# Retention attention into a top-2 expert layer on one core: gathers paced by matmuls, tail casts behind the next pair's first k cast

## The chip, the core and the metric

The kernel is one program on one core of a Trainium2 chip. The metric is the time of one execution on the device in microseconds (us), given as the median of several runs. The engines that matter are TensorE (PE, matmuls and transposes), VectorE (DVE), ScalarE (ACT), GpSimd (POOL, which also issues all indirect DMAs) and SyncE (SP, which only issues DMAs). Each engine works through its own queue in order, and engines wait for each other by semaphores.

## The reference, cut

All inputs and the output are float32. q, k and v are [8 batches, 8 heads, 576 positions, 64]. Attention has a decay in place of a softmax; its output is the input x of a noisy top-2 router and an expert layer.

```python
scores = (1 / 8) * q @ k.T                      # per batch and head
gamma = 1.0 - 2.0 ** (-5.0 - arange(8))         # per head
ret = scores * where(rel >= 0, gamma ** rel, 0) # rel = query position - key position
x = (ret @ v).transpose(0, 2, 1, 3).reshape(4608, 512)

noisy = x @ w_gate + log1p(exp(x @ w_noise)) * noise     # 8 experts
top2, weights = the two largest of noisy, softmax over these two
for e in range(8):
    h = relu(x[rows of e] @ w1[e])              # 512 -> 1024
    out[rows of e] += weight * (h @ w2[e])      # 1024 -> 512
```

## The kernel before, in words

**A planner sets the order.** The whole program is first recorded as a list of operations (`op`), each with an engine or a choice of two, a cost in microseconds, a priority and its buffers. `Plan.run` is a list scheduler: it goes through planned time, takes operations that are ready by priority, gives them buffers (`slot`) and emits each engine's instructions in that planned order. On the chip each engine then follows its queue in this order; semaphores are set from the data dependencies. The planned costs decide the order and nothing else. Buffers come in classes: `xg` (24 buffers for gathered rows, of which the expert stream may use 14 while the routing stream still needs some), `half`, `big`, PSUM banks. When the other streams of a class are done, `slot` opens the class to the one that is left: for `xg` not all at once, but 5 buffers and then one more for every two allocations (`mark`); for the other classes at once.

**Attention** runs over 16 units (a pair of batches has four: two halves of the heads by two batches), each over 512 positions. `load` (L406) fetches k, q, v through SP; `cast` (L435) scales k to bf16 on ACT (L449) or DVE (L451), and q (L457) and v (L464) with the decay, mostly on POOL; `tr` (L469) transposes on PE (L482) and copies back (`copy`: L269 on ACT, L271 on DVE); `scores` (L488, matmuls L507, mask L515); `states` (L522, matmuls L542 and L544, copies to `tb` L554 on ACT); `out_` (L561, L581 and L591). The last 64 positions of all heads of a pair of batches are its **tail** (`tail`, L604): loads by `load_tail` (L424), a k cast (L614, ACT or DVE), q and v casts (L618, DVE or POOL), transposes, scores and output of its own. There are four tails.

**Routing** (`route`, L672) follows each pair of batches, so there are four. Each writes its rows of x to a DRAM buffer `xd` (L843) and makes the list of row numbers `xi` (L823) that the gathers go by.

**Expert tiles** (`tiles`, L923). Nine early tiles of at most two row blocks of 128 use what the first three routings have found; the rest, tiles of up to four blocks ("wide"), need the last routing. `fetch` (L954) makes the gathers on POOL (L964, one indirect DMA for each block of 128 rows), then transposes on PE (L982), or for experts 6 and 7 DMA transposes (L972). `up` (L1021, matmuls L1036) and `wide` (L1049, matmuls L1062) make the first layer, with the relu L1045 on ACT or L1047 on DVE; `second` (L1113) is the second layer's matmul. `wide` interleaves the first layer of a tile with the second layer of the tile before it.

**Results.** A row gets two experts. The first one's result goes to a DRAM buffer `yd` (L1147 scales it on ACT, L1153 writes it); at the second one's turn `prev` (L1116) gathers it back on POOL (L1128), DVE adds it (L1157), and POOL scatters the sum to the output (L1161). So POOL's queue holds gathers, result gathers, scatters and the weight loads that cast on the way (L900, L904, experts 0 to 2); experts 3 to 7 load through SP (L914, L917) and are cast on ACT or DVE.

**Priorities.** Attention has its unit's number, a tail u - 0.5, a routing u - 0.4, early tile i has 100 + 4i, and the wide tiles' fetches 100 + 4i - 2, two tiles ahead.

Of the kernel before, what the change touches and what calls it, by code (L numbers as in the profile page):

```python
# [17 lines left out]
P = 128  # L18
# [4 lines left out]
DM = 512  # L23
# [6 lines left out]
YOFF = [sum(min(-(-x // P) * P, CAP) for x in FIRST[:e]) for e in range(E + 1)]  # L30
WAIT = (11, 14, 15)
CROSS = 6
CLOSE = ((256, 0, 0, 0, 0, 0, 0, 0), (512, 384, 384, 0, 0, 0, 0, 0), (768, 640, 512, 0, 0, 0, 0, 0))
PLW = 8
XW = DM // 2 + PLW
# [13 lines left out]


class Op:
    __slots__ = ("i", "eng", "fn", "prio", "dma", "port", "preds", "succ", "need", "allocs", "bufs", "fin", "on")


class Plan:
# [5 lines left out]
    BIAS = dict(DVE=1.5, ACT=0.5)  # L61

    def __init__(self):
        self.ops, self.slots, self.fifo, self.quota, self.zone, self.mark = [], {}, {}, {}, {}, {}

    def cls(self, name, tiles, **quota):
        self.slots[name] = [[0.0, None, t, p] for t, p in tiles]
# [6 lines left out]
    def fix(t=None):  # L74
        return Buf(None, None, t)

    def op(self, eng, cost, fn, r=(), w=(), prio=0.0, dma=0, after=(), port=False):
        o = Op()
        o.i, o.fn, o.prio, o.dma, o.port = len(self.ops), fn, prio, dma, port
        o.eng = eng if isinstance(eng, dict) else {eng: cost}  # L80
        o.succ, o.allocs, o.bufs = [], [], []
        preds = set(after)
        for items, wr in ((r, False), (w, True)):
            for it in items:
                b, sub = it if isinstance(it, tuple) else (it, None)
                for s2, o2, w2 in b.acc:
                    if (wr or w2) and (sub is None or s2 is None or s2 == sub):
                        preds.add(o2)
                if b not in o.bufs:
                    o.bufs.append(b)  # L90
        for items, wr in ((r, False), (w, True)):
            for it in items:
                b, sub = it if isinstance(it, tuple) else (it, None)
                if wr:
                    b.acc = [a for a in b.acc if a[1] is o or not (sub is None or a[0] == sub)]
                b.acc.append((sub, o, wr))
        preds.discard(o)
        for b in o.bufs:
            if b.cls is not None:
                if not b.ops:  # L100
                    o.allocs.append(b)
                    self.fifo.setdefault((b.cls, b.stream), []).append(b)
                b.ops.append(o)
                b.left += 1
        o.preds, o.need = preds, len(preds)
        for p in preds:
            p.succ.append(o)
        self.ops.append(o)
        return o

    def run(self):
        free, dma_free, port = {}, {}, [0.0]
        head = {k: 0 for k in self.fifo}
        used = {}
        lanes = {"SP": [], "POOL": []}
# [4 lines left out]
        def slot(b, taken):  # L120
            s = self.slots[b.cls]
            lim = self.quota[b.cls].get(b.stream, len(s))
            lo, hi = self.zone.get((b.cls, b.stream), (0, len(s)))
            if lim < len(s) and all(head[k] >= len(v) for k, v in self.fifo.items()
                                    if k[0] == b.cls and k[1] != b.stream):
                lo, hi = 0, len(s)
                n = head[b.cls, b.stream]
                lim = min(hi, 5 + (n - self.mark.setdefault((b.cls, b.stream), n)) // 2) if b.cls == "xg" else hi
            if used.get((b.cls, b.stream), 0) + sum(t[1].n for t in taken if t[1].cls == b.cls) + b.n > lim:
                return None  # L130
            ok = lambda x: x[1] is None and all(x is not y for t in taken for y in t[0])
            best = None
            for i, x in enumerate(s[:hi]):
                if i < lo:
                    continue
                if b.n == 2:
                    if i % 2 or not (ok(x) and ok(s[i + 1])):
                        continue
                    c, k = [x, s[i + 1]], (max(x[0], s[i + 1][0]), 0)
                elif not ok(x):  # L140
                    continue
                else:
                    c, k = [x], (x[0] + (0.3 if len(s) == 8 and ok(s[i ^ 1]) else 0.0), 1)
                if best is None or k < best[0]:
                    best = k, c
            return best and best[1]

        while ready:
            pick = None
            for o in ready:  # L150
# [16 lines left out]
                if not ok:  # L167
                    continue
                t0 = max([y[0] for x, b in taken for y in x], default=0.0)
                best = None  # L170
                for e, c in o.eng.items():
                    t = max(t0, free.get(e, 0.0))
# [16 lines left out]
            ready.remove(o)  # L189
            o.on = e  # L190
            free[e] = t + c
            if o.port and e in ("DVE", "POOL"):
                port[0] = t + c
            o.fin = t + c
# [39 lines left out]
class Kernel:  # L234
# [200 lines left out]
    def cast(self, u):  # L435
# [9 lines left out]
        def k(e):  # L445
# [3 lines left out]
                nc.scalar.activation(o, i, Act.Copy, scale=0.125)  # L449
            elif e == "DVE":  # L450
                nc.vector.tensor_scalar_mul(o, i, 0.125)  # L451
        pl.op({"ACT": 1.06, "DVE": 0.7}, 0, k, r=[rk], w=[kn], prio=u, port=True)

        def q(e):
            i = rq.t.rearrange("p (h r d) -> p h r d", h=4, r=4)
# [148 lines left out]
    def tail(self, bp, prio):  # L604
# [2 lines left out]
        tab, maskt, ident = (self.fixed[x] for x in ("tab", "maskt", "ident"))  # L607
        raw = {n: d["raw" + n] for n in "qkv"}
        qk, vt = pl.buf("half", "tl"), pl.buf("half", "tl")
        h8 = lambda a: a.rearrange("p (h d) -> p h d", h=E)  # L610
        qv = lambda j: qk.t.bitcast(BF16)[:, j * DM:(j + 1) * DM]
        vv = lambda: vt.t.bitcast(BF16)[:, :DM]
        pl.op({"ACT": 0.63, "DVE": 0.6}, 0,
              lambda e: nc.scalar.activation(qv(1), raw["k"].t, Act.Copy, scale=0.125) if e == "ACT"  # L614
              else nc.vector.tensor_scalar_mul(qv(1), raw["k"].t, 0.125), r=[raw["k"]], w=[(qk, 1)], prio=prio, port=True)
        for j, n, o, b in ((8, "q", lambda: qv(0), (qk, 0)), (9, "v", vv, vt)):
            pl.op({"DVE": 0.69, "POOL": 1.06}, 0,
                  lambda e, j=j, n=n, o=o: self.eng(e).tensor_tensor(  # L618
                      h8(o()), h8(raw[n].t), tab.t[:, :, j:j + 1].to_broadcast([P, E, HD]), Alu.mult),
                  r=[raw[n], tab], w=[b], prio=prio, port=True)  # L620
        pt, TT = self.psum("tl"), pl.buf("half", "tl")

        def tr(e):
# [330 lines left out]
    def fetch(self, i, t, prio):  # L954
# [6 lines left out]
        rows = 1 + 1152 * (early + 1)  # L961
        for x, j in zip(xg, js):
            h, n = HPE * e + j, self.size(j)
            pl.op("POOL", 1.3, lambda _, x=x, h=h, n=n: nc.gpsimd.indirect_dma_start(  # L964
                out=x.t[:n, :], out_offset=None, in_=self.xd[:rows, :], in_offset=IOff(ap=xi.t[:n, h:h + 1], axis=0),
                bounds_check=rows - 1, oob_is_err=False), r=[xi] + self.xd_done[early], w=[x], prio=prio, dma=0.4)
        xT = pl.buf("half" if early < 3 else "big", "xt")
        w, m, off = sum(self.size(j) for j in js), len(js) * P, self.off(js)
        xv = lambda m=m: xT.t.bitcast(BF16)[:, :KD * m].rearrange("p (k s) -> p k s", k=KD)
# [79 lines left out]
    def wide(self, i, t, prio, g2=None):  # L1049

        pl, nc = self.pl, self.nc
        w, d = self.W[t[0]], self.t[i]
        n, xT, xv = d["w"], d["xT"], d["xv"]
        hT = d["hT"] = [pl.buf("half", "exp") for _ in range(4)]
        for f in range(KF):
            p = self.psum("exp")

            def pe(_, f=f, p=p):
                it = g2(f) if g2 else iter(())
                for di in range(KD):  # L1060
                    o = di * F + f * P
                    nc.tensor.matmul(p.t[:, :n], lhsT=w.t[:, o:o + P], rhs=xv()[:, di, :n],  # L1062
                                     start=(di == 0), stop=(di == KD - 1))
                    next(it, None)
                for _ in it:
                    pass
            r, ww, c = [xT] + [(w, k) for k in range(KD)], [p], 0.435 * n / 256
            if g2:
                r2, w2, c2 = g2.deps(f)
                r, ww, c = r + r2, ww + w2, c + c2  # L1070
            pl.op("PE", c, pe, r=r, w=ww, prio=prio)
            hv = lambda f=f: hT[f // 2].t.bitcast(BF16).rearrange("p (f s) -> p f s", f=2)[:, f % 2, :n]
            op = pl.op({"ACT": 0.17 + 0.00084 * n, "DVE": 0.1 + 0.00115 * n}, 0, lambda g, p=p, hv=hv: self.relu(
                g, hv(), p.t[:, :n]), r=[p], w=[(hT[f // 2], f)], prio=prio)
            if g2:
                for s in g2.ends(f):
                    self.finish(i - 1, g2.t, s, prio)
        return op
# [28 lines left out]
    def second(self, e, po, hT, c, f):  # L1107
# [2 lines left out]
        k = KF // len(hT)  # L1110
        hv = hT[f // k].t.bitcast(BF16).rearrange("p (f s) -> p f s", f=k)[:, f % k]
        o = KD * F + f * DM
        self.nc.tensor.matmul(po.t, lhsT=hv[:, c:c + P], rhs=self.W[e].t[:, o:o + DM],  # L1113
                              start=(f == 0), stop=(f == KF - 1))

    def prev(self, i, t, prio):  # L1116
        pl, nc = self.pl, self.nc
# [52 lines left out]

    def record(self):
        pl = self.pl
        self.u, self.tails, self.T, self.xT, self.W, self.t, self.keep, self.scats, self.wdma, self.inps = {}, {}, {}, {}, {}, {}, {}, {}, [], []
        self.setup()
        for u in range(3):
            self.load(u)
# [27 lines left out]
        for i, t in enumerate(ts):  # L1204
            starts.setdefault(t[0], i)
        last = {t[0]: i for i, t in enumerate(ts)}
        ne = len([t for t in ts if t[2] < 3])
        landed = lambda u: [o for o in pl.ops if o.dma and o.prio == u]
        for e, u in enumerate(WAIT):
            self.weights(e, 40 + e, True, landed(u))  # L1210
# [200 lines left out]
```

## Time and profile before

| | |
|---|---|
| median of 3 runs | 490.4 us (485.36, 490.4, 490.55) |
| the profiled execution's own time | 485.52 us |
| its span in the profile | 484.0 us |
| mean TensorE clock granted | 0.926 |
| busy: PE, DVE, ACT, POOL | 398.0 us (82%), 187.5 (39%), 246.4 (51%), 292.9 (61%) |
| gathers L964 on POOL | 80, of 1045 ns each |
| scatters L1161 and result gathers L1128 | 39 of 1003 ns, 39 of 1022 ns |
| matmuls L1062 and L1113 | 640 each, 190.5 us and 214.9 us busy |
| first matmul of a wide tile (L1062) | starts at 227.70 us |
| last matmul | ends at about 474 us |

A line of the profile names the kernel's line (L964), the engine, the instruction, and output and input by the program's names. "<-" in brackets or behind a bar names what ended the engine's idle time ahead of an instruction: an engine and its instruction, a DMA, "issue" (nothing that the profile shows), or "remote" (a semaphore update for which the profile finds no instruction). The clock is a share of TensorE's full speed.

### The profile page before, as it was taken

The numbers are of one execution on the slowest core, as the hardware profiler recorded it, in microseconds if no ns is written. First come the engines' busy times: TensorE is split into PE (matmuls) and PEld (weight loads), VectorE is DVE, ScalarE is ACT, GpSimd is POOL, SyncE is SP. The second block draws the span as 40 slices with busy tenths as digits, with TensorE's granted clock in tenths as the row PEclk, the third lists the DMA queues.
The fourth block names the chain that finished last, engine by engine and source line by source line (L and its number), as shares of the span: only waits on it lengthen the run. The fifth ranks groups of instructions, "written<-read, shape, count | busy, mean of one in ns | idle before, by whom it ended". The sixth has DMA issues, their size and how long they took to land. (4 is left out here: it accounts for less than half of the span.)

```text
span 484.0 us, 10610 instructions
## 1 busy us (share of the span) xinstructions
PE 398.0 (82%) x4032; PEld 245.5 (51%) x4032; DVE 187.5 (39%) x499; ACT 246.4 (51%) x431; POOL 292.9 (61%) x361
## 2 busy tenths in 40 slices
PE   1698768729988898149999888999799979999991
PEld 1576657528766665026565434455354434454450
DVE  2755776855892782001133313215025021031231
ACT  3699758657874743026575354745345233244320
POOL 8985779874497365733007747544656746656524
PEclk9889769878999999569999989999999979999997
DMA  7999999999599595423189977695599996645414
GB/s 192 298 261 286 272 238 303 257 245 328 128 319 269 136 256 166 96 75 118 37 291 349 343 248 220 188 369 166 167 310 298 236 217 182 181 150 161 150 55 144
DMA packets 102488, 105.32 MB, mean 218 GB/s; under 512 B 31870, under 2 KB 80511, under 8 KB 102434
## 3 DMA queue, kind: packets, MB, share of 16 engines
q1 hardware_dynamic: 80082, 58.92, 41.8%
q0 software_dynamic: 15264, 36.89, 30.2%
q10 hardware_dynamic: 7088, 8.80, 5.2%
q8 instruction: 32, 0.52, 0.5%
q14 instruction: 22, 0.18, 0.1%
HBM read 83.20 MB, written 26.63 MB: 227 GB/s over the span
## 5 line engine op out<-in xcount | busy, mean ns | idle before, releaser
L1113 PE MATMUL ps<-W,half 128*128 128x512 bf16 x640 | 214.9, 388 | 24.6 <-ACT half L1045 18.1
L1062 PE MATMUL ps<-big,W 128*128 128x512 bf16 (+4 forms) x640 | 190.5, 331 | 5.8 <-issue 5.2
L1045 ACT ACTIVATE half<-ps 128x512 bf16<-128x512 f32 (+5 forms) x180 | 87.1, 505 | 158.2 <-PE ps L1062 70.2
L964 POOL DMA_INDIRECT xg<-xd,xi x80 | 83.6, 1045 | 57.0 <-issue 20.4
L1113 PEld LDWEIGHTS <-half 128*128 128x128 bf16 x640 | 62.2, 99 | 99.4 <-ACT half L1045 18.9
L1062 PEld LDWEIGHTS <-W 128*128 128x128 bf16 x640 | 63.1, 99 | 55.5 <-issue 9.1
L1157 DVE SCALAR_TENSOR_TENSOR half<-ps,xg,half 128x512 f32<-128x512 f32 (+1 forms) x39 | 29.0, 747 | 73.5 <-PE ps L1113 42.1
L1161 POOL DMA_INDIRECT out_dram<-half,xg x39 | 39.1, 1003 | 29.6 <-issue 16.6
L1128 POOL DMA_INDIRECT half<-yd,xg x39 | 39.8, 1022 | 11.9 <-issue 11.9
L515 DVE TENSOR_TENSOR half<-ps,mask 128x512 bf16<-128x512 f32 x64 | 40.1, 682 | 16.4 <-PE ps L507 14.4
L269 ACT ACTIVATE half<-ps 128x1024 bf16<-128x1024 bf16 (+1 forms) x36 | 35.1, 990 | 15.5 <-PE ps L482 9.3
L457 POOL TENSOR_TENSOR half<-big,tab 128x1024 bf16<-128x1024 f32 x16 | 31.0, 1935 | 14.6 <-PE ps L482 6.2
L464 POOL TENSOR_TENSOR half<-big,tab 128x512 bf16<-128x512 f32 x32 | 33.6, 1066 | 1.5 <-issue 1.5
L542 PE MATMUL ps<-half,half 128*128 128x128 bf16 (+1 forms) x128 | 30.2, 322 | 2.4 <-POOL half L464 2.2
L1157 DVE SCALAR_TENSOR_TENSOR half<-ps,gm,half 128x512 f32<-128x512 f32 x6 | 4.5, 751 | 70.9 <-ACT half L1147 64.4
L1036 PE MATMUL ps<-half,W 128*128 128x256 bf16 (+1 forms) x288 | 29.1, 255 | 2.9 <-ACT half L269 2.5
L482 PE MATMUL ps<-ident__69,half 128*128 128x128 bf16 x256 | 22.3, 247 | 11.0 <-ACT half L449 5.9
L544 PE MATMUL ps<-vz,half 128*128 128x128 bf16 x128 | 25.4, 251 | 6.3 <-ACT vz L269 4.6
L1147 ACT ACTIVATE half<-ps,xg 128x512 f32<-128x512 f32 (+1 forms) x29 | 19.9, 685 | 16.4 <-PE ps L1113 11.0
L1036 PEld LDWEIGHTS <-W 128*128 128x128 bf16 x288 | 24.0, 98 | 7.0 <-issue 3.4
L554 ACT ACTIVATE tb<-ps 64x256 bf16<-64x256 f32 x56 | 21.1, 376 | 11.0 <-PE ps L544 9.8
L482 PEld LDWEIGHTS <-half 128*128 128x128 bf16 x256 | 18.9, 113 | 12.0 <-ACT half L449 5.9
(177 smaller groups left out, 462.8 us busy)
## 6 DMA issues: line engine op xcount, KB each, us to landing
big<-in_moe_w_dram SPq DMA_DIRECT2D x40, 512.0 KB
big<-in_k_dram SPq DMA_DIRECT2D x32, 256.0 KB
big<-in_q_dram SPq DMA_DIRECT2D x16, 512.0 KB
big<-in_v_dram SPq DMA_DIRECT2D x32, 256.0 KB
yd<-half SPq DMA_DIRECT2D x26, 256.0 KB
W<-in_moe_w_dram POOLq DMA_DIRECT2D x12, 512.0 KB
xd<-xg ACTq DMA_DIRECT2D x16, 264.0 KB
yd<-half ACTq DMA_DIRECT2D x15, 256.0 KB
```

The lines of the kernel that those rows point to most:

```text
L269: self.nc.scalar.activation(out, in_, Act.Copy)
L464: self.eng(e).tensor_tensor(o, i, t, Alu.mult)
L482: nc.tensor.transpose(v[:, hp, x, :], i[:, y, hp * P:(hp + 1) * P], ident.t)
L515: nc.vector.tensor_tensor(S.t.bitcast(BF16).rearrange("p (h c x) -> p h c x", h=2, c=2)[:, h], p[h].t.rearrange("p (c x) -> p c x", c=2), ...
L964: pl.op("POOL", 1.3, lambda _, x=x, h=h, n=n: nc.gpsimd.indirect_dma_start(out=x.t[:n, :], out_offset=None, in_=self.xd[:rows, :], in_offs ...
L1036: nc.tensor.matmul(pv()[:, f2, :], lhsT=w.t[:, o:o + P], rhs=xv()[:, di, :n], start=(di == 0), stop=(di == KD - 1))
L1045: self.nc.scalar.activation(o, i, Act.Relu)
L1062: nc.tensor.matmul(p.t[:, :n], lhsT=w.t[:, o:o + P], rhs=xv()[:, di, :n], start=(di == 0), stop=(di == KD - 1))
L1113: self.nc.tensor.matmul(po.t, lhsT=hv[:, c:c + P], rhs=self.W[e].t[:, o:o + DM], start=(f == 0), stop=(f == KF - 1))
L1128: pl.op("POOL", 1.3, lambda _, b=b, iy=iy, n=self.size(j): nc.gpsimd.indirect_dma_start(out=b.t[:n, :], out_offset=None, in_=self.yd[:rows ...
L1157: pl.op("DVE", 0.75, lambda _, o=o, b=b, po=po, g=g, n=n: nc.vector.scalar_tensor_tensor(o.t[:n], po.t[:n], g()[:n], b.t[:n], Alu.mult, Al ...
L1161: ins = nc.gpsimd.indirect_dma_start(out=self.out[:, :], out_offset=IOff(ap=io()[:n], axis=0), in_=o.t[:n, :], in_offset=None, bounds_chec ...
```

## The change

Four edits; nothing is added to or taken from the computation.

1. **Pace in the planner.** An operation may carry a `pace`. Such an operation is planned to start at the earliest 2.2 us (`PACE`) of planned time after the paced one before it.
2. **Gathers wait for matmuls.** The gathers of all wide tiles but the first are paced, and each gets a semaphore dependency on the last expert matmul of `wide` (L1062) or `second` (L1113) that was emitted before it (`self.mm`).
3. **Buffers.** The `mark` rule goes: when the routings have taken their last `xg` buffer, all 24 are open to the expert stream at once.
4. **Tail casts.** The k, q and v casts of a tail depend on the k cast of the next pair's first unit (`late`), for the first three tails; the last has no next pair.

```diff
+PACE = 2.2
 ...
-                n = head[b.cls, b.stream]
-                lim = min(hi, 5 + (n - self.mark.setdefault((b.cls, b.stream), n)) // 2) if b.cls == "xg" else hi
+                lim = hi
 ...
+                if o.pace:
+                    t0 = max(t0, paced + o.pace)
 ...
+            if o.pace:
+                paced = t
 ...
-        pl.op({"ACT": 1.06, "DVE": 0.7}, 0, k, r=[rk], w=[kn], prio=u, port=True)
+        self.kcast[u] = pl.op({"ACT": 1.06, "DVE": 0.7}, 0, k, r=[rk], w=[kn], prio=u, port=True)
 ...
+        late = [self.kcast[u] for u in (4 * bp + 4,) if u in self.kcast]
 ...
-              else nc.vector.tensor_scalar_mul(qv(1), raw["k"].t, 0.125), r=[raw["k"]], w=[(qk, 1)], prio=prio, port=True)
+              else nc.vector.tensor_scalar_mul(qv(1), raw["k"].t, 0.125), r=[raw["k"]], w=[(qk, 1)], prio=prio, port=True,
+              after=late)
 ...
-                  r=[raw[n], tab], w=[b], prio=prio, port=True)
+                  r=[raw[n], tab], w=[b], prio=prio, port=True, after=late)
 ...
+            pace = PACE if early == 3 and i > self.ne else 0.0
+
+            def get(_, x=x, h=h, n=n, pace=pace):
+                ins = nc.gpsimd.indirect_dma_start(
 ...
+                if pace:
+                    self.tc.add_manual_dep(ins.ins, self.mm.ins.name, mybir.DependencyInfo(
+                        mybir.DependencyClass.Sync, mybir.DependencyReason.DATA), reason="gathers go at TensorE's pace")
+            pl.op("POOL", 1.3, get, r=[xi] + self.xd_done[early], w=[x], prio=prio, dma=0.4, pace=pace)
 ...
-                    nc.tensor.matmul(p.t[:, :n], lhsT=w.t[:, o:o + P], rhs=xv()[:, di, :n],
-                                     start=(di == 0), stop=(di == KD - 1))
+                    self.mm = nc.tensor.matmul(p.t[:, :n], lhsT=w.t[:, o:o + P], rhs=xv()[:, di, :n],
+                                               start=(di == 0), stop=(di == KD - 1))
 ...
-        self.nc.tensor.matmul(po.t, lhsT=hv[:, c:c + P], rhs=self.W[e].t[:, o:o + DM],
-                              start=(f == 0), stop=(f == KF - 1))
+        self.mm = self.nc.tensor.matmul(po.t, lhsT=hv[:, c:c + P], rhs=self.W[e].t[:, o:o + DM],
+                                        start=(f == 0), stop=(f == KF - 1))
```

(`self.ne` is the number of early tiles, nine; `early == 3` marks the tiles that need the last routing.) In the order that results, the first wide tile's four gathers and the next one stand back to back on POOL, the others singly or in runs with scatters and result gathers of at most about seven indirect DMAs. Some instructions of other stages move too: the transposes of the tile after the second routing stand ahead of the last attention units on PE, one of its gathers ahead of two weight loads on POOL and the other behind them, and on ACT the third tail's k cast stands behind the k cast of unit 12, the `vz` copy, four `tb` copies and a transpose copy.

More of the change, by code (lines that the diff above doesn't have):

```diff
@@ L51 @@
 class Op:
-    __slots__ = ("i", "eng", "fn", "prio", "dma", "port", "preds", "succ", "need", "allocs", "bufs", "fin", "on")
+    __slots__ = ("i", "eng", "fn", "prio", "dma", "port", "preds", "succ", "need", "allocs", "bufs", "fin", "on", "pace")
 class Plan:
@@ L63, in __init__ @@
     def __init__(self):
-        self.ops, self.slots, self.fifo, self.quota, self.zone, self.mark = [], {}, {}, {}, {}, {}
+        self.ops, self.slots, self.fifo, self.quota, self.zone = [], {}, {}, {}, {}
     def cls(self, name, tiles, **quota):
@@ L75, in fix, with op @@
         return Buf(None, None, t)
-    def op(self, eng, cost, fn, r=(), w=(), prio=0.0, dma=0, after=(), port=False):
+    def op(self, eng, cost, fn, r=(), w=(), prio=0.0, dma=0, after=(), port=False, pace=0.0):
         o = Op()
-        o.i, o.fn, o.prio, o.dma, o.port = len(self.ops), fn, prio, dma, port
+        o.i, o.fn, o.prio, o.dma, o.port, o.pace = len(self.ops), fn, prio, dma, port, pace
         o.eng = eng if isinstance(eng, dict) else {eng: cost}
@@ L111, in run @@
     def run(self):
-        free, dma_free, port = {}, {}, [0.0]
+        free, dma_free, port, paced = {}, {}, [0.0], 0.0
         head = {k: 0 for k in self.fifo}
@@ L963, in fetch @@
             h, n = HPE * e + j, self.size(j)
-            pl.op("POOL", 1.3, lambda _, x=x, h=h, n=n: nc.gpsimd.indirect_dma_start(
-                out=x.t[:n, :], out_offset=None, in_=self.xd[:rows, :], in_offset=IOff(ap=xi.t[:n, h:h + 1], axis=0),
-                bounds_check=rows - 1, oob_is_err=False), r=[xi] + self.xd_done[early], w=[x], prio=prio, dma=0.4)
+            pace = PACE if early == 3 and i > self.ne else 0.0
+            def get(_, x=x, h=h, n=n, pace=pace):
+                ins = nc.gpsimd.indirect_dma_start(
+                    out=x.t[:n, :], out_offset=None, in_=self.xd[:rows, :], in_offset=IOff(ap=xi.t[:n, h:h + 1], axis=0),
+                    bounds_check=rows - 1, oob_is_err=False)
+                if pace:
+                    self.tc.add_manual_dep(ins.ins, self.mm.ins.name, mybir.DependencyInfo(
+                        mybir.DependencyClass.Sync, mybir.DependencyReason.DATA), reason="gathers go at TensorE's pace")
+            pl.op("POOL", 1.3, get, r=[xi] + self.xd_done[early], w=[x], prio=prio, dma=0.4, pace=pace)
         xT = pl.buf("half" if early < 3 else "big", "xt")
@@ L1172, in record @@
         pl = self.pl
-        self.u, self.tails, self.T, self.xT, self.W, self.t, self.keep, self.scats, self.wdma, self.inps = {}, {}, {}, {}, {}, {}, {}, {}, [], []
+        self.u, self.tails, self.T, self.xT, self.W, self.t, self.keep, self.scats, self.wdma, self.inps, self.kcast = {}, {}, {}, {}, {}, {}, {}, {}, [], [], {}
         self.setup()
@@ L1206, in record @@
         last = {t[0]: i for i, t in enumerate(ts)}
-        ne = len([t for t in ts if t[2] < 3])
+        self.ne = ne = len([t for t in ts if t[2] < 3])
         landed = lambda u: [o for o in pl.ops if o.dma and o.prio == u]
```

## Prediction

> **What bounds the kernel now.** First the page: span, slices and the costliest groups.
>
> ```profile
> span 484.0 us, 10610 instructions
> ...
> PE   1698768729988898149999888999799979999991
> ...
> POOL 8985779874497365733007747544656746656524
> PEclk9889769878999999569999989999999979999997
> ...
> L1045 ACT ACTIVATE half<-ps 128x512 bf16<-128x512 f32 (+5 forms) x180 | 87.1, 505 | 158.2 <-PE ps L1062 70.2
> L964 POOL DMA_INDIRECT xg<-xd,xi x80 | 83.6, 1045 | 57.0 <-issue 20.4
> ```
>
> A slice is 12.1 us. TensorE (PE) is full almost everywhere behind slice 18; slices 17 and 18 (194 to 218 us) show 1 and 4 tenths and a clock of 5 and 6 tenths, with POOL at 7. So PE sets the end, and the question is what empties it there. The waits between 184 and 212 us (engine, line, waited for: total, times, longest) and those of the wide tiles, 227 to 474 us, name it:
>
> ```profile
> ACT half L1045 <- remote: 19.4, 3, 7.9
> ...
> PE ps L1113 <- ACT half L1045: 14.8, 2, 7.4
> ```
>
> ```profile
> ACT half L1045 <- remote: 18.7, 4, 8.5
> ```
>
> "Remote" means a semaphore update for which the profile finds no instruction. The timeline of 184 to 228 us, ACT then PE then POOL (start, duration, in brackets the idle time before):
>
> ```profile
> 194.31 0.60 ACT L1045 ACTIVATE half<-ps 128x512 bf16<-128x512 f32 x1 [3.72 <-remote]
> 202.78 0.60 ACT L1045 ACTIVATE half<-ps 128x512 bf16<-128x512 f32 x1 [7.86 <-remote]
> 211.23 1.08 ACT L1045 ACTIVATE half<-ps 128x512 bf16<-128x512 f32 x2 [7.86 <-remote]
> ```
>
> ```profile
> 191.40 0.49 PE L1036 MATMUL ps<-half,W 128*128 128x256 bf16 x3 [0.35 <-issue]
> ...
> 211.88 4.18 PE L1113 MATMUL ps<-W,half 128*128 128x512 bf16 x12 [7.42 <-ACT half L1045]
> ...
> 219.40 3.62 PE L1113 MATMUL ps<-W,half 128*128 128x512 bf16 x16
> ```
>
> ```profile
> 193.34 0.95 POOL L964 DMA_INDIRECT xg<-xd,xi  x1 [0.31 <-issue]
> 194.59 1.00 POOL L964 DMA_INDIRECT xg<-xd,xi  x1 [0.30 <-issue]
> ...
> 217.06 1.00 POOL L964 DMA_INDIRECT xg<-xd,xi  x1 [1.30 <-ACT half L1147]
> ...
> 224.00 1.00 POOL L964 DMA_INDIRECT xg<-xd,xi  x1 [0.73 <-ACT half L1147]
> ```
>
> The early tile's L1036 matmuls are done by 191.9, yet the relus that evict them (L1045) start at 194.3, 202.8 and 211.2. From 184.26 to 208.59 POOL issues 19 gathers (L964) back to back, 1.0 us each with 0.30 between. While it does, ACT learns of PE's finished matmuls up to 8 us late. At 217.06 and later, where gathers have gaps of 1.3 us and more, the next relu follows its matmul after 0.3 to 0.4 us; behind the gap of 0.73 at most 0.9 us was lost. My reading: PE's completion signals get through only when POOL's run of indirect DMAs breaks. The trace shows the coincidence, not the mechanism. The size is in the windows (length, busy time of PE, PEld, DVE, ACT, POOL, PE clock, DMA share, GB/s):
>
> ```profile
> 192.00:212.00 20.00, 2.19 (x5) 0.39 (x6) 0.52 (x4) 1.96 (x4) 12.89 (x13) 0.56 0.35 88
> 212.00:227.70 15.70, 15.70 (x124) 9.96 (x124) 0.98 (x5) 8.10 (x15) 3.98 (x4) 0.91 0.32 102
> ...
> 340.00:400.00 60.00, 54.09 (x276) 26.27 (x275) 13.07 (x19) 22.70 (x44) 36.69 (x36) 0.94 0.96 245
> ```
>
> 17.8 of 20 us are lost; then PE is full up to the first wide matmul (L1062) at 227.70. One more hole lies in the attention phase, on ACT:
>
> ```profile
> 99.38 0.63 ACT L614 ACTIVATE half<-half 128x512 bf16<-128x512 f32 x1 [6.75 <-DMA half<-in_k_dram]
> ```
>
> The cast of the third tail's k waits 6.75 us for its load. Behind it in ACT's queue stand the next pair's cast of k (L449, its data had landed by 88), four state copies (L554) and copies of transposes (L269); PE's L507 waits 8.5 us for one of these, until 106.34.
>
> **The change, part by part.**
>
> (1) Tail casts behind the next pair's first cast of k. No instruction is added. In the changed kernel's order ACT runs, ahead of that L614, the k cast (1.04 us), the vz copy (1.04), the L554 group (1.54) and a transpose copy (1.02). So at most 4.7 us of the 6.75 are filled; at worst nothing, when PE's other inputs are as late. I take 3, most of the upper end, since PE's wait was on just such a copy. The first two tails show no such wait: 0.
>
> (2) Paced gathers. Of 80 gathers 61 are paced. After the last routing the first wide tile's four and one more still go back to back (5 x 1.3 = 6.5 us), then single ones 2.2 us apart, a gap of 1.2 us, near the 1.30 that was prompt. Removed: 17.8 us idle, and 1.5 us of slow clock behind it (12 matmuls in 4.18 are 348 ns each, 16 in 3.62 are 226; 12 x 0.122). Left over: some lateness in the first five, between 0 and 6.5; I take 2, since PE still had 4 to 5 us of matmuls at that point. Net -17.3 (bounds -12.8 to -19.3). What is late next: nothing at once. The first wide tile would start at about 210; its gathers are out by 191 and one issued at 190.73 was read at 194.90; a wide tile takes PE (474 - 227.7)/20 = 12.3 us, while the next tile's four gathers need 4 x 2.2 = 8.8.
>
> (3) The wide tiles. Their idle PE time is 4.1 (270 to 300 us), 2.1 (300 to 340) and 5.9 (340 to 400); 400 to 474 is full (73.95 of 74). The four "remote" waits of 18.7 us stand inside dense runs of gathers and scatters (263 to 280, 371 to 390). In the new order runs are of about seven DMAs at most (7 x 1.3 = 9.1 us), so shorter, not gone. Bounds 0 and 13 (12.1 plus 1 of slow clock); I take 4, a third.
>
> (4) The added semaphore wait itself. A paced gather waits for the last L1062 or L1113 matmul ahead of it in the order. Queued behind it on POOL are the scatters (L1161), the gathers of earlier results (L1128) and weight loads; L1157 on DVE waits for L1128, PE's banks for L1157. The cost is nothing while POOL has slack: in 340 to 400 us it is busy 36.7 of 60, so 23.3 us idle in 4.9 tiles, 4.8 per tile; 3.25 gathers at 1.2 us of gap use 3.9. That is tight (the first rival).
>
> (5) All 24 gather buffers open at once (the rule that let them grow one for two is gone): it only moves the order, which the pacing then sets; 0.
>
> (6) Order changes elsewhere. The transposes of the tile that follows the second routing now stand ahead of the last attention units on PE, and one of its gathers ahead of two weight loads on POOL, the other behind them. Before, a gather issued behind such loads at 131.16 was read at 139.07. If PE waits for that in its queue, up to 8 us; PE has about 6 us idle in 130 to 190 to absorb it. Bounds 0 to 8, I take 2.
>
> **Sum**, on the profiled execution: 484.0 - 3 - 17.3 - 4 + 2 = 461.7 us of span; 1.5 us lie around it (485.52 - 484.0), so 463.2. The runs shown are 485.36, 490.4 and 490.55: the profiled one stands with the fastest, 4.9 below the median. I add 1.8, a good third of that, for a median of the same kind: **465**.
>
> **The rivals.**
>
> A. Head of line (slower). The wait of (4) outgrows POOL's slack. Place: POOL's queue in the wide phase. Each tile's first paced gather is held until PE is far enough, PE is held for a bank that L1157 frees, L1157 for an L1128 behind that gather. It decides once the waits pass 4.8 us per tile. At 2.5 us beyond, over 20 tiles, it costs 50: 461.7 + 50 + 1.5 = 513; over ten tiles 488. For it: slack and need are 4.8 and 3.9. Against: the matmul waited for is one that stands earlier in the order, so no closed loop, and POOL is idle at the places where gathers are now put.
>
> B. The signals are late for another reason, so spacing does nothing: 484.0 - 3 + 2 + 1.5 = 484.5. For it: only coincidence is shown. Against: all seven long "remote" waits lie in dense runs, none in sparse ones. The Trainium skill ("Trainium Architecture — The Big Picture", section "What this means for kernel authors") states that the engines are independent and that one does not block another without a semaphore between them. By that rule POOL's gathers could not hold up PE's signal to ACT, and this rival's time would hold; the 7.86 us rows above speak against it here.
>
> C. Most of the order is worse: the tail gains 0, the routing comes 2 to 8 us later, the wide phase gains nothing, the start gains only 12.8: 484.0 - 12.8 + 8 + 1.5 = 480.7 at the worst, 470 at the milder end. For it: the last routing's work and three attention units move back in the order.
>
> D. All late signals go: 484.0 - 4.7 - 19.3 - 13 + 1.5 = 448.5. Against: runs of five to seven DMAs stay.
>
> **How the numbers follow.** Forecast (455 to 472) 0.52, C 0.16, D 0.12, A 0.13, B 0.07. Three runs of this kernel spread by 1%, so 1% is about what can be told from no change. Forecast, D and C are faster by more than that (0.80, and 0.02 of B's), the rest of B is the same (0.05), A is slower (0.13). The range, 448 to 483, holds all but A and B and the outer ends.
>
> **What would show it.** Right: no "remote" wait over 3 us between 184 and 212; PE full there and the first wide matmul near 210 to 213; single L964 rows on POOL some 2.2 us apart with idle time before them put down to PE; L614 of the third tail started with little wait, and PE's L507 wait down from 8.5 to about 5. Wrong: the remote waits still there (B); long L964 waits for PE followed by L1157 waiting for the L1128 load and PE for L1157 (A); the last routing more than 3 us later than before (C).

## The result and the profile after

The changed kernel takes 472.81 us (median of 4 runs, 471.41 to 473.41) where the kernel before takes 488.17 (median of 4, 485.36 to 490.55): a ratio of 0.971, interval 0.967 to 0.976. It is faster, by 15 us, where 465 was forecast. The profiled execution took 473.4 us with a span of 471.9. Where the runs of one kernel in one session lie more than 1.5% apart, a ratio uses the faster runs alone; this is so only for the kernel before in the session of e11 and e12 (479.47, 480.73 and 486.06 of seven runs from 479.47 to 491.69).

The lines of the page that answer to those of before (L1059, L1050, L1076 and L1127 are the old L1045, L1036, L1062 and L1113; L974 is the gather, L273 the old L269):

```profile
span 471.9 us, 10634 instructions
...
PE   1686868683785979999969999799999979999991
...
POOL 8985579884098735244453737366666667657524
PEclk9999779998797979999998999899999999999997
...
L974 POOL DMA_INDIRECT xg<-xd,xi x80 | 82.9, 1036 | 82.1 <-ACT half L1059 23.6
```

The hole behind the last routing (slices 17 and 18 before) is gone, and so is the slow clock there. New ones stand at slice 10 (106 to 118 us), slice 13 (142 to 153 us) and slice 21. In the windows the stretch that was 2.19 us of PE in 20 is full (PE, PEld, DVE, ACT, POOL, clock, DMA share, GB/s):

```profile
192.00:212.00 20.00, 19.96 (x166) 14.09 (x164) 6.22 (x20) 11.66 (x20) 9.02 (x9) 1.00 0.48 145
```

The timeline of that stretch, POOL first, then ACT, shows how: the gathers have gaps, ended by PE's or ACT's work, and the relu starts 0.4 us behind its matmul:

```profile
207.11 1.00 POOL L974 DMA_INDIRECT xg<-xd,xi  x1 [1.58 <-PE ps L1127]
209.32 0.95 POOL L974 DMA_INDIRECT xg<-xd,xi  x1 [1.21 <-ACT half L1161]
```

```profile
205.29 0.60 ACT L1059 ACTIVATE half<-ps 128x512 bf16<-128x512 f32 x1 [0.41 <-PE ps L1050]
```

But more lines of the timeline tell what was lost ahead of it. The first gather behind the last routing, before and then after, and the first wide matmul after:

```profile
184.26 0.96 POOL L964 DMA_INDIRECT xg<-xd,xi  x1 [5.45 <-DVE half L1047]
```

```profile
196.47 1.05 POOL L974 DMA_INDIRECT xg<-xd,xi  x1 [9.35 <-DVE nov__63 L1392]
```

```profile
221.08 6.38 PE L1076 MATMUL ps<-big,W 128*128 128x448 bf16 x33
```

The first gather goes at 196.47, where it went at 184.26: 12.2 us later. From there to the first wide matmul it takes 24.6 us in place of 43.4 (-18.8), so the wide phase starts 6.6 us earlier; from its start to the end of the span it takes 250.8 in place of 256.3 (-5.5). Together -12.1, the difference of the spans (484.0 to 471.9).

A loss is seen first in the attention phase, on ACT and then on PE:

```profile
114.19 5.20 ACTq L850 DMA_DIRECT2D xd<-xg  x4
119.44 1.06 ACT L273 ACTIVATE vz<-half 64x1024 bf16<-64x1024 bf16 x1 [10.53 <-DMA xd<-xg]
```

```profile
120.55 0.26 PE L548 MATMUL ps<-vz,half 128*128 128x128 bf16 x1 [9.14 <-ACT vz L273]
```

ACT has the writes of the second routing's rows in its queue (L850, the old L843; "ACTq" is its issuing of DMAs). It stands from 108.9 to 119.4 at them, and PE waits 9.14 us for the `vz` copy behind. Before, PE had waited 8.48 us for a copy behind the third tail's cast:

```profile
106.34 1.07 PE L507 MATMUL ps<-half,half 64*64 64x128 bf16 x32 [8.48 <-ACT half L269]
```

One wait took the place of the other, at almost the same size. So when the third routing begins, the change is only 1.4 us behind. POOL's product with the noise (L702, now L709), before and then after:

```profile
127.75 0.34 POOL L702 TENSOR_TENSOR nl<-nl,noise 128x72 f32<-128x72 f32 x1 [4.58 <-ACT nl L701]
```

```profile
129.11 0.34 POOL L709 TENSOR_TENSOR nl<-nl,noise 128x72 f32<-128x72 f32 x1 [14.47 <-ACT nl L708]
```

The other 10.9 us arise between there and the first gather behind the last routing: 67.4 us in place of 56.5, with nearly the same number of matmuls (735 and 728). In that stretch POOL issues five gathers and two weight loads almost without a gap (161.94 to 169.86), and ACT stands until their end:

```profile
169.83 1.02 ACT L273 ACTIVATE xg<-ps 128x1024 bf16<-128x1024 bf16 x1 [4.16 <-remote]
```

### The profile page after: what moved, and what is told of

It reads as the page before. It is cut to its first block, busy times and chain, and to the rows that moved or that the text cites. A ratio compares the mean times of both kernels' runs of the same rounds, so it can differ in the third digit from the quotient of the medians.

```text
span 471.9 us, 10634 instructions
## 1 busy us (share of the span) xinstructions
PE 397.3 (84%) x4032; PEld 247.8 (53%) x4032; DVE 187.2 (40%) x499; ACT 249.7 (53%) x432; POOL 289.2 (61%) x360
## 5 line engine op out<-in xcount | busy, mean ns | idle before, releaser
L1127 PE MATMUL ps<-W,half 128*128 128x512 bf16 x640 | 212.9, 385 | 3.1 <-issue 1.6
L1076 PE MATMUL ps<-big,W 128*128 128x512 bf16 (+4 forms) x640 | 190.1, 331 | 3.3 <-DVE big L275 2.5
L1059 ACT ACTIVATE half<-ps 128x512 bf16<-128x512 f32 (+5 forms) x178 | 86.2, 504 | 129.6 <-PE ps L1076 70.3
L974 POOL DMA_INDIRECT xg<-xd,xi x80 | 82.9, 1036 | 82.1 <-ACT half L1059 23.6
L1127 PEld LDWEIGHTS <-half 128*128 128x128 bf16 x640 | 62.9, 99 | 74.4 <-issue 8.2
L1076 PEld LDWEIGHTS <-W 128*128 128x128 bf16 x640 | 63.1, 99 | 52.0 <-issue 5.6
L273 ACT ACTIVATE half<-ps 128x1024 bf16<-128x1024 bf16 (+1 forms) x33 | 32.5, 1001 | 17.5 <-PE ps L486 12.9
L461 POOL TENSOR_TENSOR half<-big,tab 128x1024 bf16<-128x1024 f32 x15 | 28.6, 1904 | 7.9 <-DMA big<-in_q_dram 6.3
L1161 ACT ACTIVATE half<-ps,xg 128x512 f32<-128x512 f32 (+1 forms) x33 | 22.7, 687 | 14.8 <-PE ps L1127 13.3
L1050 PE MATMUL ps<-half,W 128*128 128x256 bf16 (+1 forms) x288 | 29.9, 259 | 0.4 <-ACT half L273 0.4
L486 PEld LDWEIGHTS <-half 128*128 128x128 bf16 x256 | 18.2, 111 | 17.5 <-POOL half L461 8.3
L1050 PEld LDWEIGHTS <-W 128*128 128x128 bf16 x288 | 24.4, 99 | 5.0 <-issue 0.6
L546 PEld LDWEIGHTS <-half 128*128 128x128 bf16 x128 | 14.2, 111 | 23.8 <-issue 20.3
L273 ACT ACTIVATE xT<-ps 128x512 bf16<-128x512 f32 (+1 forms) x40 | 20.0, 554 | 9.3 <-POOL half L625 7.1
```

The lines of the kernel that those rows point to most:

```text
L273: self.nc.scalar.activation(out, in_, Act.Copy)
L486: nc.tensor.transpose(v[:, hp, x, :], i[:, y, hp * P:(hp + 1) * P], ident.t)
L546: nc.tensor.matmul(o[:, 2 * c + 1:, :], lhsT=kk[:, r, c, y], rhs=m, start=(c == 0 and r == 0), stop=False, skip_group_check=True)
L974: ins = nc.gpsimd.indirect_dma_start(out=x.t[:n, :], out_offset=None, in_=self.xd[:rows, :], in_offset=IOff(ap=xi.t[:n, h:h + 1], axis=0), ...
L1050: nc.tensor.matmul(pv()[:, f2, :], lhsT=w.t[:, o:o + P], rhs=xv()[:, di, :n], start=(di == 0), stop=(di == KD - 1))
L1059: self.nc.scalar.activation(o, i, Act.Relu)
```

## The experiments

Each session's runs share a chip and the runs of the kernel before. The sessions fall into two kinds, told apart by the time of before itself: 445 to 446 us in three of them, 480 to 488 in the last one and in the runs above. In the first kind no trace has a remote wait over 1.1 us; in the second kind every trace has some of 4 to 9 us ("late signals" below). The table says which; comparisons are made inside a session or through before.

| run | kernel | this | before there | ratio |
|---|---|---|---|---|
| the case | change | 472.81 | 488.17 | 0.971 (0.967 to 0.976) |
| e1 | tail edit alone | 459.68 | 445.75 | 1.030 (1.025 to 1.035) |
| e2 | all but the tail edit | 450.59 | 445.75 | 1.011 (1.005 to 1.017) |
| e3 | all but the added wait | 452.70 | 445.75 | 1.016 (1.011 to 1.021) |
| e4 | added wait alone | 461.74 | 445.75 | 1.036 (1.032 to 1.040) |
| e5 | before | 445.60 | 445.50 | 1.001 (0.998 to 1.004) |
| e6 | change | 457.98 | 445.50 | 1.030 (1.026 to 1.034) |
| e7 | spaced plan, no wait, no tail edit | 445.59 | 445.50 | 1.001 (0.997 to 1.005) |
| e8 | buffer rule alone | 448.58 | 445.50 | 1.007 (1.004 to 1.010) |
| e9 | e3, row writes on POOL | 444.43 | 446.38 | 0.993 (0.990 to 0.996) |
| e10 | e7, row writes on POOL | 444.49 | 446.38 | 0.996 (0.993 to 0.999) |
| e11 | change, row writes on POOL | 465.56 | 480.73 (487.38 of all seven) | 0.966 (0.957 to 0.976) |
| e12 | e11, wait on the first tiles only | 473.06 | 480.73 (487.38 of all seven) | 0.982 (0.970 to 0.995) |

### One part at a time: e1 to e4

**e1, the tail edit alone.** The kernel before with this:

```diff
+        late = [self.kcast[u] for u in (4 * bp + 4,) if u in self.kcast]
...
-              ... r=[raw["k"]], w=[(qk, 1)], prio=prio, port=True)
+              ... r=[raw["k"]], w=[(qk, 1)], prio=prio, port=True, after=late)
```

> Edit 4 alone on the kernel before: tail casts behind the next pair's first k cast; no pace, no added wait, the old buffer rule. Its order up to the last routing is that of the changed kernel. Theory 1 (the tail edit moves the transposes ahead of the last attention units and so costs about 12 us at the last routing, and the dense gathers behind it still hold PE for some 17 us): first gather behind the last routing near 196, remote waits of 7 to 8 us as before, time about 496 (492 to 500), slower than before. Rival (the tail edit gains its 3 us, and the 12 us late routing came from the pacing): about 482, first gather near 181.

Measured: 14 us slower than before, the direction of theory 1, but before itself was 40 us faster here than in the runs above. The first gather behind the last routing goes at 189.60, where theory 1 had it near 196. The trace has no remote wait, though its gathers run back to back, 21 of them (timeline, POOL and then ACT):

```profile
202.67 1.00 POOL L975 DMA_INDIRECT xg<-xd,xi  x1 [0.31 <-issue]
203.97 1.00 POOL L975 DMA_INDIRECT xg<-xd,xi  x1 [0.30 <-issue]
```

```profile
204.03 0.60 ACT L1057 ACTIVATE half<-ps 128x512 bf16<-128x512 f32 x1 [0.28 <-PE ps L1048]
```

So a dense run of gathers does not by itself make PE's signals late. That half of theory 1 fell, as it was worded.

**e2, the change without the tail edit.**

```diff
-        late = [self.kcast[u] for u in (4 * bp + 4,) if u in self.kcast]
+        late = []
```

> Edits 1 to 3 without edit 4. Theory 1: the attention phase is that of before, the first gather behind the last routing goes at about 184, no remote wait over 3 us behind it, the first wide matmul at about 210, time 461 (457 to 465), 11 below the changed kernel. Rival (the tail edit is worth its 3 us): about 476, slower than the changed kernel.

Measured: 5 us slower than before; 450.59 was under both theories' figures, which were made for the other level. First gather at 184.50, first wide matmul at 206.86: the late routing is gone with the tail edit.

**e3, the change without the added wait.**

```diff
-                if pace:
-                    self.tc.add_manual_dep(ins.ins, self.mm.ins.name, ...)
```

> The changed kernel without the added wait: same order on every engine, gathers only planned 2.2 us apart. Theory 1 (dense runs of gathers on POOL hold PE's signals back; order alone leaves nothing on POOL between two gathers, so they run densely): 20 or more gathers back to back from 196, remote waits of 7 to 8 us again, time 485 to 492. Rival (the order and not the wait does it): remote waits stay away, 473.

Measured: 7 us slower than before. Its gathers are dense again, as expected, and no signal is late (one remote wait, of 1.04 us), so it could not tell wait and order apart.

**e4, the added wait alone**, in the old order with the old buffer rule.

> The kernel before with the added wait of the wide tiles' gathers on the last expert matmul and nothing else: old order, gathers planned densely. Theory 1: a late PE holds the gathers back, which breaks the run, so the remote waits shrink to 3 us or less and the time falls to about 470 (464 to 476). Rival A (the wait without spacing in the order blocks scatters and result gathers): 485 or more. Rival B (lateness has another cause): 484 to 486 with the remote waits unchanged.

Measured: 16 us slower, the direction of rival A, whose figure was made for the other level. The gathers of one of the first wide tiles were held until PE stood at that tile (POOL's waits in the whole run, then PE's timeline):

```profile
POOL xg L975 <- ACT half L1060: 17.5, 13, 11.1
POOL xg L975 <- PE ps L1128: 15.3, 10, 7.4
```

```profile
237.53 0.34 PE L1077 MATMUL ps<-big,W 128*128 128x192 bf16 x1 [9.88 <-DVE big L276]
```

The wait needs the spaced order: with the dense one, a gather is tied to a matmul far too late for it.

### Before and after again: e5 to e8

> The kernel before, unchanged, for its trace beside those of the other experiments. Theory 2 (formed after the first four: the late signals are not a property of dense gathers alone, since a run of 21 gathers back to back in e1 let the relus start 0.3 us behind their matmuls; they belong to the chip or its state): on a chip without them no remote wait over 3 us, PE full behind the last routing, first wide matmul near 208, 445. Where the chip has them: 485 to 490 and the three waits of 4 to 8 us.

Measured: 445.60, the very program that took 488. It has the same dense run, 25 gathers from 182.59, and relus behind their matmuls at once:

```profile
188.86 0.60 ACT L1045 ACTIVATE half<-ps 128x512 bf16<-128x512 f32 x1 [0.28 <-PE ps L1036]
```

First wide matmul at 204.79 (227.70 in the first profile), wide phase 238.7 us (256.3). Between the two traces of this one program lie 40.5 us: 22.9 and 17.6. The faster trace has no remote wait; the waits of the whole slower one are of that size:

```profile
ACT half L1045 <- remote: 38.2, 7, 8.5
```

> The changed kernel, unchanged. Theory 2: without the late signals there is nothing for pacing to win, and the tail edit's late routing stays: about 455 (451 to 460) against 446 before, slower. Theory 1 (it is faster wherever it runs): below 446. On a chip with late signals: 471 to 474 against 485 to 490.

Measured: 457.98. Without late signals the change is 3% slower, as theory 2 said (455 was expected). The four traces by stretch, in us:

| stretch | before, late signals | before, none (e5) | change, late signals | change, none (e6) |
|---|---|---|---|---|
| start to the first gather behind the last routing | 184.3 | 182.6 | 196.5 | 189.4 |
| from there to the first wide matmul | 43.4 | 22.2 | 24.6 | 24.0 |
| from there to the end of the span | 256.3 | 238.7 | 250.8 | 241.8 |

Between its two sessions the kernel before differs by 40.5 us (1.7, 21.2 and 17.6), the change by 16.7 (7.1, 0.6 and 9.0). So the change takes away 23.8 us of late signals and pays 11.7 for it, which e6 beside e5 shows (6.8, 1.8 and 3.1). It also meets late signals in a new place, ahead of the last routing: 7.1 us where before lost 1.7.

**e7, the spaced plan and the freed buffers**, with neither wait nor tail edit, and **e8, the buffer rule alone:**

```diff
-                lim = min(hi, 5 + (n - self.mark.setdefault((b.cls, b.stream), n)) // 2) if b.cls == "xg" else hi
+                lim = hi
```

> The kernel before with the spaced plan and the freed buffers, but neither the added wait nor the tail edit. If the added wait is what costs the 5 us of e2, 446 or below; if the spaced order costs them, 450. On a chip with late signals: the gathers run densely again and 480 to 488 is expected.

> The kernel before with the buffer rule alone taken away (24 gather buffers open at once). Without late signals: within 1% of before, 442 to 449, since the gathers of the first wide tiles all come in time either way. With late signals: a run of up to 24 gathers in place of 19, 485 to 495.

Measured: e7 445.59, no different from before, so e2's 5 us are the added wait's. e8 448.58, 3 us slower; the spaced plan wins these back. By these runs the change's 12.4 us in e6 are 7 for the tail edit (e3 beside e7) and 5 for the wait (e2 beside e7; e6 beside e3 gives 5.5). Alone the tail edit cost 14 (e1): beside e5's trace 9.1 of these lie ahead of the first wide matmul (213.88) and 6.1 behind it, where e3, in the spaced plan, has 237.1 us beside e5's 238.7.

### What the tail edit costs: e9 and e10

The list of the built program shows four of the five row writes with a wait each on one of eight DMA semaphores, which the loads of SP's queue use in turn; so such a write waits until an earlier load has landed. With the tail edit the four stand in a row directly ahead of the `vz` copy; before, three of them stood farther ahead of it. The test leaves the order of PE, DVE and SP as it is and takes only the writes out of ACT's way:

```diff
-            pl.op("ACT", 0.4, lambda e, n=n, xr=xr, row=row: nc.scalar.dma_start(
+            pl.op("ACT", 0.4, lambda e, n=n, xr=xr, row=row: (nc.gpsimd if bp == 1 else nc.scalar).dma_start(
```

> The kernel of e3 (tail edit, spaced plan, no added wait) with one thing changed: the second routing's five writes of rows to xd are issued from POOL's queue in place of ACT's, at the same place in the plan; the order on PE, DVE and SP is e3's. Theory 3 (the tail edit costs its 7 us because ACT, in order, stands some 10 us at these writes, which wait for earlier loads, and PE then waits 8.8 us for the vz copy behind them): PE's wait for vz falls below 3 us, the first wide matmul comes at about 207 in place of 214, and the time is 446 to 448 beside 445.6 of before. Rival (the transposes of the next early tile standing ahead of the last attention units cost it): still 451 to 454.

> The control for e9: the kernel of e7 (spaced plan, no added wait, no tail edit) with the same five writes issued from POOL. Theory 3: ACT did not stand long at these writes here, so little changes: 443 to 447. If the move itself wins or loses more than 3 us, e9 has to be read against this.

Measured: e9 444.43, 2 us under before where e3 was 7 above, and below the 446 to 448 of theory 3; e10 444.49, 2 under. PE's waits in e3, then in e9:

```profile
PE ps L548 <- ACT vz L273: 13.4, 5, 8.7
```

```profile
PE ps L548 <- ACT vz L273: 4.9, 4, 1.8
```

The first wide matmul moves from 214.28 to 206.46. So moving the writes takes away all that the tail edit costs in the end; the rival, whose transposes stand there in e9 too, fails as it was worded. With the writes moved the tail edit is worth nothing in total (e9 and e10 agree), though in e10 the third tail's cast still waits 5.9 us for its load. The two traces show why: e9 is 5.9 us ahead of e10 at the third routing (L709 at 120.43 and 126.36) and takes 6.8 longer from there to the first gather behind the last one (62.4 and 55.6). So a gain and a loss of the tail edit cancel. PE's waits for a gather in front of those transposes are 1.4 us of the loss (L993 in e9); what causes the rest was not tested.

### The added wait where signals are late: e11 and e12

e11 is the whole change with the writes moved; e12 has the added wait only on the paced gathers of the first four wide tiles behind the first:

```diff
-                if pace:
+                if pace and i <= self.ne + 4:
```

> The whole changed kernel with the second routing's five writes of rows issued from POOL (e9 plus the added wait on all 61 paced gathers). If the parts add up (tail edit 0 once the writes are moved, added wait 4 to 5 in the wide phase): 449 (447 to 451) beside 446 of before, first wide matmul near 206 as in e9. If the wait costs nothing by itself and e2's 5 us came from elsewhere: 444 to 445. On a chip with late signals: about 460 beside 488.

> e11 with the added wait on the paced gathers of the four wide tiles behind the first alone, so that the run behind the last routing is broken and the later gathers are free. If the wait's cost lies in the later wide tiles, where POOL also has scatters and result gathers in its queue: 444 to 446, as e9. If it lies in the first tiles (gathers that come too late for the next tile): 448 to 450, as e11.

These two runs met the late signals, on the same chip as e5 to e8. e11: 465.56, 7 under the change in the other such session, and 15 under before; about 460 was expected for this level. e12: 473.06, 7.5 slower than e11, with the same order on PE and POOL. Their first wide matmuls come together (211.89 and 211.21), so the difference lies behind. The waits in e12, then in e11:

```profile
ACT half L1059 <- remote: 16.7, 5, 7.6
DVE half L1171 <- remote: 9.1, 2, 8.9
DVE half L1061 <- remote: 8.1, 1, 8.1
```

```profile
DVE half L1171 <- remote: 5.2, 1, 5.2
...
ACT half L1059 <- remote: 2.6, 2, 1.7
```

Where the wait is taken off, POOL runs densely again (in e12 from 246.3 to 260.5 without a gap over 0.31 us), and a relu behind that run starts 7.62 us late; before the late relu the profile again names no instruction:

```profile
262.08 0.44 ACT L1059 ACTIVATE half<-ps 128x320 bf16<-128x320 f32 x1 [7.62 <-remote]
```

One factor, one session: breaking the runs of indirect DMAs takes away most of the late signals (36 us of remote waits on ACT and DVE in e12, 8 in e11). Not all: e11's wide phase is 252.4 us (260.6 in e12), where the change without late signals takes 241.8. The same wait costs 5 us where no signal is late. Which of e12's expectations holds on the other level was not measured.

e11 is the fastest version seen in the sessions with late signals; e9 and e10, without the wait, in the others, where they are 0.7% and 0.4% under before. e9 with late signals and e11 without them were not run.

## Why the prediction was right or wrong

**What bounds the kernel: right for this state of the machine.** The stall behind the last routing is late signals while gathers run densely. e12 beside e11 shows the link, where the prediction had a coincidence. Its wording, that signals get through only when POOL's run breaks, does not fit its own rows: the relus at 194.31 and 202.78 start inside the unbroken run and the third one 2.6 us behind its end. What it did not know is that the state comes and goes with the session: e5 is the same program with such a run and no stall. That the result was measured in a session with late signals is luck for the sign of the forecast; in e6 the same change lost 12 us.

**(2), the pacing: right.** -17.3 was forecast, -18.8 measured from first gather to first wide matmul, inside the bounds. The five unpaced gathers cost less than the 2 us set aside: no relu in 192 to 212 had a remote wait. Mostly single gathers, gaps of 1.2 us and more, PE full: as written.

**(3), the wide tiles: right in sign, -5.5 for -4.** Late signals stay there, shorter (7.0 us at the longest, on DVE). By the table of e6 they cost 9.0 us there in place of 17.6, and 3.1 of the gain go to the change's own price. Of the four waits that the step placed in 263 to 280 and 371 to 390, two short ones (2.25 us each) end elsewhere, at 348.31 and 450.31.

**(1), the tail casts: failed.** -3 was forecast. The third tail's cast did wait less for its load, 1.29 us in place of 6.75, and PE's wait of 8.48 us on L269 did go; but a later unit's scores (L507, now L511) start at 126.27 in place of 124.92. The step filled ACT's hole with work and did not look at what ACT reaches next: the row writes, which stand in ACT's queue too and wait for loads. With these moved (e11) the third routing comes 7.2 us ahead of before (120.56 and 127.75), more than the 3 forecast, and the stretch behind it loses that again.

**(6), the order elsewhere: mis-sized.** +2 was taken, with bounds of 0 and 8; the last routing came 12.2 us late. Moving the row writes, a cause that the step did not name, takes 8.4 of it away (196.47 to 188.05 in e11; 190.49 in e3 to 182.78 in e9 without late signals). What is left is 3.8 with late signals and 0.9 without (182.78 in e9, 181.93 in e10); each is the sum of a gain ahead of the third routing and a larger loss behind it. The wait that the step did name, PE's transposes (L996) for those gathers, is 1.2 us in the case. The 139.07 of its working stands in no row: the first transpose of a gathered row (L982) behind 131.16 that the trace has starts at 144.76. With the writes out of the way the change takes 465.56, beside the 465 forecast, but this is in part luck: its span is 464.3 where the sum gave 461.7, and the terms differ.

**(4), the added wait: taken as nothing, and hidden.** Where signals are late its gain covers it. Where they are not, it costs 5 us, a tenth of rival A's price, and by the traces 4.1 (e2 beside e7) to 4.7 (e6 beside e3) arise in the wide phase. Rival A's mechanism was seen whole only in e4, and there it was the gathers themselves that came late, not the scatters behind them.

**(5), the freed buffers: 0 was taken.** Alone they cost 3 us (e8), with the spaced plan nothing (e7).

**Rival B** (spacing does nothing, 484.5) is refuted here by e11 and e12. The rule of the Trainium skill that stood beside it ("Trainium Architecture — The Big Picture", section "What this means for kernel authors"), that the engines are independent, fits the sessions without late signals (e5) and not the others. **Rival C** had the right place, the routing, and a delay of 2 to 8 us. The measured 472.81 lies just above the forecast's own band (455 to 472) and in C's (470 to 480.7); the chance C was given, 0.16, was low for what happened, but it counted the start's gain too small.

## What to carry to other kernels

Before filling an engine's wait with later work, follow its queue to the next instruction that can block, DMA issues included: a write that waits for somebody else's load holds all the compute behind it, and moving five such writes to POOL's queue won 9 us where the edit itself won none (e9 beside e3 and e10). A wait that paces DMA issues belongs with an order that leaves room for it; alone it cost 16 us. And a stall whose end the profile puts down to nothing in the program should be measured in a second session before a change is built on it: this change is 3% faster in one kind of session and 3% slower in the other.

## What was not expected of the hardware

The same program on the same chip took 445 us in one session and 479 to 492 in another. In the slower sessions PE's completions reach ACT and DVE up to 8.9 us late. These waits lie in or just behind runs of indirect DMAs that POOL issues back to back (1.0 us each, 0.30 between); gaps of 1.2 us and more let the relus through in 0.4 us. PE's own stream is slowed too in at least one place: beside the same five gathers the sixteen L665 and eight L669 matmuls of the last tail take 2.7 us in the case (167.37 to 170.06) and 0.7 in e6 (164.02 to 164.71). In the other sessions a run of 25 such DMAs delayed nothing (0.28 us). What sets the state was not found: the chip does not (e5 and e11 ran on one), nor does the kernel. Whether the late signals come from the gathers' issuing or from something that the machine shares with other work was not tried.
